# Summing the second layer's early partial attention groups with 32-column weights, under another table of planner thresholds

## The chip, the cores and the metric

The kernel runs on one core of one Trainium2 chip. The core has a matrix engine (TensorE, PE in the profile, its weight loads PEld), a vector engine (VectorE, DVE), an activation engine (ScalarE, ACT), a general engine (GpSimd, POOL) and a queue that issues transfers (SyncE, SP). The metric is device microseconds of one execution; the time of a kernel is the median of its runs.

## The reference

Four layers on 2048 tokens of width 512, all in bfloat16, each added to its input after a layer norm: A, B, A, B. Both kinds have 32 heads of width 16.

```
A: per segment of 512 tokens: p = softmax(causal(q k^T / 4)); a_dot = p v
   o = sigmoid(beta) * a_mem + (1 - sigmoid(beta)) * a_dot
   a_mem = (phi(q) M) / (phi(q) z); then M += phi(k)^T v, z += sum phi(k)
B: p = softmax(q k^T / 4) over all 2048 keys; o = p v
x = x + A(ln(x)); x = x + B(ln(x)); x = x + A(ln(x)); x = x + B(ln(x))
```

## The kernel before

The whole program is written by a planner (`Builder`) that runs before the launch. It keeps an estimated clock for each engine (`Sched.estimate`, line 95), decides from these clocks what to issue next, and so fixes the order of the instructions on every engine; on the chip each engine works through its list and waits on semaphores. Layers are numbered L = 0 to 3; 0 and 2 are of kind A, 1 and 3 of kind B.

**Groups and banks.** Attention is cut into groups (`Group`, made in `make_groups`, line 1363): one layer, one segment of 512 queries, one chunk of 8 heads, and every second head of it (`e` is 0 or 1), so 4 heads. Scores are made as blocks of 128 keys by 512 queries of one head, one PSUM bank each (the code calls the pair of key block and head a bank): 64 for a whole group of kind B. In layer 1 the groups of the first query segment (`qseg` 0) are cut into four waves, one for each key segment, of 16 banks each, since the keys of later segments come late out of layer 0. That makes 32 partial groups, which run in three stretches between the segments of layer 0. Layer 3 cuts its first query segment into two waves in the same way.

**A unit** (`unit`, line 1454) takes two or three banks. TensorE makes the scores with 32-row weights (four heads lie in four row strips: tiles `ps<-qm,KB`), ScalarE takes the exponential of two or three banks in one instruction into `pT` (line 1514), and two units later TensorE multiplies the exponentials with the values and sums over keys into one accumulator bank (`pv`, line 1556). The values have 16 columns and a column of ones, so the sum of the exponentials comes out as the 17th.

**The share of VectorE.** For some banks the exponential is approximated on VectorE instead: one eviction to 16-bit integers (`dx_first`, line 1121) and two or three shifts of these (`dx_shift`, line 1184), each of which gives one more term that `pv` must sum. Which banks go this way, when, and in what order is decided by thresholds of the planner (`dx_room`, `dx_find`, `dx_most`).

**Two forms of the sum.** In the narrow form the exponentials are the weights (128 by 128) and the values stream, so that a bank takes four matmuls of 50 or 52 columns, with the queries on the partitions; a finished group is divided by its sums, written to `ob` and brought to `oT` by a DMA transpose. In the wide form (`g.fm`) the values are the weights (17 columns, in a 32-column strip of the array that is picked by the head's place `r`), the exponentials stream, and a bank takes one matmul of 512 columns; queries lie on the free axis, and VectorE transposes the finished sums in blocks of 32 (`finish_fm`, line 1634) and transposes the output of two groups again into `oT` (line 1674). The form is picked by

```
self.fm = kind == "B" and Builder.FM >= (1 if L == 3 and first and last else
          2 if L == 3 else 3 if first and last else 4)                 # line 252
```

With `FM` = 3 all of layer 3 and the whole groups of layer 1 (query segments 1 to 3) are wide; the 32 partial groups of layer 1 are narrow.

**Partial sums** (`finish`, line 1592). At the end of each wave the accumulator is added by VectorE into an SBUF area (`accS`: tiles `KB` or `VB`): a copy at the first wave (line 1604), an addition after (line 1606), over 272 columns in the narrow form and 512 in the wide one. Until it has been read, the next group's sums cannot start in the accumulator.

**Background.** Layer norms, projections, output projections and the memory of kind A are tasks that the planner slips between units (`background`, line 1316) by credits and by how far each engine's clock is ahead. Projections go through one PSUM bank, which ScalarE or VectorE evicts (`evac`, line 475). Where TensorE has little to do, `keep_busy` (line 429) adds matmuls of zeros.

**The table.** `PIECES` (line 271) is a list of times on the planner's ScalarE clock, one each 40 us from 20 us on; when the clock passes a time, the thresholds named there are set (line 1810) and hold until they are set again. Among them are how many banks VectorE may take (`TAKEN`, `REST`, `NEAR_S`), how far clocks may drift (`MARGIN`, `SLACK`, `DVE_LATE`), the credits per unit (`CR_W`, `PE_B`) and the zeros (`FILL`, `FILLS`).

Of the kernel before, what the change touches and what calls it, by code (L numbers as in the profile page):

```python
# [257 lines left out]
class Builder:  # L258
    NPU, NDX, FIT, MARGIN, PART, FILL_DVE, EARLY, FILL = 4, 5, 2, 450, 1, 300, 700, 0.5
    FILLS, DVE_FIN, DX_FIN, EVAC_ACT, DX_BANK, DX_LATE, BG_BANK, DVE_LATE = 2, 600, 2000, 0, 500, 3000, 200, 1000  # L260
    DVE_LATE_LOW, CR_A, CR_B, CR_W, CR_LOW, CARRY, CARRY_W, REST = 9000000000.0, 1300, 1500, 1400, 1900, 0, 0, 11
    NEAR, SLACK, ALT3, ALT5, GAP, AHEAD, PE_B, PE_A = 10, 300, 2, 4, 2, 300, 4, 5
    PE_LOW, LOW, PAIRS, TAKEN, PAIRS2, NKS, DX_T, POOL_T = 6, 24, 40, 2.7, 1, 6, 430, 2900
    POOL_ON, DQN, TAKEN_N, REST_N, NEAR_N, NEAR_W, DQ, DXS = 0, 600, 3, 14, 130, 8, 2200, 1
    PVN, PVLATE, PVWAIT, PVHOLE, DMA_STEPS, DMA_LATE, DXA, DXA_REST = 4, 900, 0, 100, 2, 600, 0, 10
    DXA_N, DXA_W, APARTS, FILL_NEAR, FILL_FREE, HOR, PHI, QUAD = 13, ('k0', 'k13'), ('k2', 'k13', 'k0'), 0, 1, 400, 'kq', ('in', 1, 3)
    QREST, CLOSE, FM, NAREA, XDX, NEAR_S, NEAR_E, DX_WAIT = 24, ('proj', 2, 2), 3, 18, 99, 60, 60, 400
    DX_RES, CHAINS, ALT, ALTS, ALTA = 0, 4, 0, 3, (1, 1, 1, 1)
    ORDER = [[(-4.6, 7.7, 7.6, 0.9, -10), (3.8, -10.8, 0.4, 20, -10.8), (19, 59.6, 22, 59.8, 12), (31, 44.3, 46.9, 10.6, 0.2)],
             [(-1.5, -6.7, -5.8, 20.8, 1.2), (-5.2, -1.6, 28.5, 28, 7), (21, 35.0, 8.2, 30, 27.7), (21, 48.0, 37, 23.6, 12.2)]]  # L270
    PIECES = [(20.0, {'DXA_REST': 14, 'EVAC_ACT': -300, 'LOW': 32}),
              (60.0, {'AHEAD': 500, 'CR_W': 1900, 'DXA_REST': 10, 'EVAC_ACT': -300, 'LOW': 24, 'wide': True}),
              (100.0, {'AHEAD': 500, 'CR_W': 1900, 'DQ': 1900, 'EVAC_ACT': -300, 'wide': True}),
              (140.0, {'AHEAD': 300, 'CR_W': 1400, 'DQ': 2200, 'DX_T': 480, 'EVAC_ACT': 0}),
              (180.0, {'DMA_LATE': 300, 'DX_FIN': 2500, 'DX_T': 480, 'PE_B': 5, 'PE_LOW': 5}),
              (220.0, {'DMA_LATE': 600, 'DX_FIN': 2000, 'DX_T': 430, 'LOW': 16, 'PE_B': 4, 'PE_LOW': 6, 'PVN': 6}),
              (260.0, {'DX_RES': 2, 'HOR': 100, 'LOW': 24, 'NEAR_N': 200, 'PVN': 4}),
              (300.0, {'DX_RES': 2, 'HOR': 100, 'MARGIN': 700, 'NEAR_N': 200}),
              (340.0, {'DMA_LATE': 300, 'DQ': 1900, 'DX_RES': 2, 'FILLS': 1, 'HOR': 100, 'MARGIN': 700, 'NEAR_E': 80, 'NEAR_N': 200}),
              (380.0, {'DMA_LATE': 300, 'DMA_STEPS': 3, 'DQ': 2500, 'DX_RES': 2, 'DX_T': 330, 'FILLS': 1, 'HOR': 100, 'MARGIN': 700, 'NEAR_E': 0, 'NEAR_N': 200}),  # L280
              (420.0, {'DMA_LATE': 300, 'DMA_STEPS': 3, 'DQ': 2500, 'DX_RES': 2, 'DX_T': 330, 'FILLS': 1, 'HOR': 100, 'MARGIN': 700, 'NEAR': 6, 'NEAR_E': 0, 'NEAR_N': 200}),
              (460.0, {'ALTA': (1, 9, 9, 9), 'DMA_LATE': 300, 'DMA_STEPS': 3, 'DQ': 2500, 'DX_RES': 2, 'DX_T': 330, 'FILLS': 1, 'HOR': 100, 'MARGIN': 700, 'NEAR': 10, 'NEAR_E': 0, 'NEAR_N': 200, 'TAKEN': 1.5}),
              (500.0, {'ALTA': (1, 1, 9, 9), 'CR_W': 1250, 'DMA_LATE': 600, 'DMA_STEPS': 2, 'DQ': 2200, 'DQN': 300, 'DX_RES': 0, 'DX_T': 430, 'FILLS': 2, 'HOR': 400, 'MARGIN': 450, 'NEAR_E': 60, 'NEAR_N': 130, 'TAKEN': 2.7}),
              (540.0, {'ALTA': (1, 1, 1, 1), 'CR_W': 1400, 'DQ': 2500, 'DQN': 600, 'PE_A': 4}),
              (580.0, {'DQ': 2200, 'FILLS': 1, 'FILL_DVE': 450, 'PART': 3, 'PE_A': 5}),
              (620.0, {'FILLS': 1, 'FILL_DVE': 450, 'NEAR_S': 30, 'PART': 3, 'SLACK': 150}),
              (660.0, {'FILLS': 2, 'FILL_DVE': 300, 'NEAR_S': 60, 'PART': 1, 'SLACK': 0}),
              (700.0, {'MARGIN': 700, 'SLACK': 0, 'TAKEN': 2.4}),
              (740.0, {'DQ': 2500, 'DX_LATE': 1500, 'MARGIN': 700, 'SLACK': 0, 'TAKEN': 2.4}),
              (780.0, {'DQ': 2200, 'DX_LATE': 3000, 'MARGIN': 450, 'PVHOLE': 250, 'PVLATE': 600, 'SLACK': 300, 'TAKEN': 2.7}),  # L290
              (820.0, {'BG_BANK': 0, 'PVHOLE': 100, 'PVLATE': 900, 'TAKEN': 3}),
              (860.0, {'AHEAD': 200, 'BG_BANK': 200, 'TAKEN': 2.7}),
              (900.0, {'AHEAD': 200, 'DX_LATE': 1500, 'DX_RES': 1}),
              (940.0, {'AHEAD': 200, 'DX_LATE': 1500, 'DX_RES': 1, 'FILL_DVE': 150, 'MARGIN': 700}),
              (980.0, {'AHEAD': 200, 'DX_LATE': 1500, 'DX_RES': 1, 'FILL_DVE': 150, 'MARGIN': 700, 'REST': 14}),
              (1020.0, {'AHEAD': 200, 'DVE_FIN': 1000, 'DX_LATE': 1500, 'DX_RES': 1, 'FILL_DVE': 150, 'MARGIN': 700, 'PART': 3, 'REST': 14}),
              (1060.0, {'AHEAD': 300, 'CARRY_W': 300, 'DVE_FIN': 600, 'DX_LATE': 3000, 'DX_RES': 0, 'FILL': 0.35, 'FILL_DVE': 300, 'MARGIN': 450, 'PART': 1, 'REST': 11, 'REST_N': 20}),
              (1100.0, {'CARRY_W': 300, 'DMA_STEPS': 3, 'DXA_REST': 26, 'FILL': 0.35, 'LOW': 4, 'REST_N': 20}),
              (1140.0, {'CARRY_W': 0, 'DMA_STEPS': 2, 'DXA_REST': 10, 'FILL': 0.5, 'FILLS': 3, 'LOW': 4, 'PVN': 3, 'REST_N': 14}),
              (1180.0, {'FILLS': 3, 'LOW': 4, 'NEAR_S': 30, 'PVN': 2}),  # L300
              (1220.0, {'FILLS': 3, 'LOW': 4, 'MARGIN': 700, 'NEAR_S': 30, 'PVN': 2}),
              (1260.0, {'DVE_FIN': 1000, 'FILLS': 3, 'LOW': 4, 'MARGIN': 700, 'NEAR_S': 30, 'PVN': 2}),
              (1300.0, {'AHEAD': 200, 'BG_BANK': 400, 'DVE_FIN': 1000, 'DX_RES': 1, 'FILLS': 3, 'FILL_DVE': 150, 'LOW': 4, 'MARGIN': 700, 'NEAR_S': 30, 'PVN': 2}),
              (1340.0, {'AHEAD': 200, 'BG_BANK': 400, 'DVE_FIN': 1000, 'DX_RES': 1, 'FILL': 0.45, 'FILLS': 3, 'FILL_DVE': 150, 'LOW': 4, 'MARGIN': 700, 'NEAR_S': 30, 'PVN': 2}),
              (1380.0, {'AHEAD': 200, 'BG_BANK': 400, 'DVE_FIN': 1000, 'DX_RES': 1, 'FILL': 0.45, 'FILLS': 3, 'FILL_DVE': 150, 'LOW': 4, 'MARGIN': 700, 'NEAR_S': 30, 'PVN': 2}),
              (1420.0, {'AHEAD': 200, 'BG_BANK': 400, 'DVE_FIN': 1000, 'DX_RES': 1, 'FILL': 0.45, 'FILLS': 3, 'FILL_DVE': 150, 'LOW': 4, 'MARGIN': 700, 'NEAR_S': 30, 'PVN': 2}),
              (1460.0, {'AHEAD': 200, 'BG_BANK': 400, 'DVE_FIN': 1000, 'DX_RES': 1, 'EVAC_ACT': -300, 'FILL': 0.45, 'FILLS': 2, 'FILL_DVE': 150, 'LOW': 4, 'MARGIN': 700, 'NEAR_S': 30, 'PVN': 2, 'REST': 14, 'REST_N': 20}),
              (1500.0, {'AHEAD': 200, 'BG_BANK': 400, 'DVE_FIN': 1000, 'DX_RES': 1, 'EVAC_ACT': -300, 'FILL': 0.45, 'FILL_DVE': 150, 'LOW': 4, 'MARGIN': 700, 'NEAR_S': 30, 'PVN': 2, 'REST': 14, 'REST_N': 20}),
              (1540.0, {'AHEAD': 200, 'BG_BANK': 400, 'DVE_FIN': 1000, 'DX_RES': 1, 'EVAC_ACT': -300, 'FILL': 0.45, 'FILL_DVE': 150, 'LOW': 4, 'MARGIN': 700, 'NEAR_S': 30, 'PVN': 2, 'REST': 11, 'REST_N': 20}),
              (1580.0, {'AHEAD': 200, 'BG_BANK': 400, 'DVE_FIN': 1000, 'DX_RES': 0, 'EVAC_ACT': -300, 'FILL': 0.45, 'FILL_DVE': 150, 'LOW': 4, 'MARGIN': 700, 'NEAR_S': 30, 'PVN': 2, 'REST': 5, 'REST_N': 20, 'TAKEN': 3.5}),  # L310
              (1620.0, {'AHEAD': 200, 'BG_BANK': 400, 'DVE_FIN': 1000, 'EVAC_ACT': -300, 'FILL': 0.45, 'FILL_DVE': 150, 'LOW': 4, 'MARGIN': 700, 'NEAR_S': 30, 'PVN': 2, 'REST': 5, 'REST_N': 20, 'TAKEN': 3.5}),
              (1660.0, {'AHEAD': 300, 'BG_BANK': 200, 'DVE_FIN': 600, 'DX_T': 530, 'EVAC_ACT': 0, 'FILL': 0.5, 'FILL_DVE': 300, 'LOW': 24, 'MARGIN': 450, 'NEAR_N': 200, 'NEAR_S': 60, 'PVN': 4, 'REST': 11, 'REST_N': 14, 'TAKEN': 3, 'TAKEN_N': 4}),
              (1700.0, {'DVE_FIN': 1000, 'DX_T': 530, 'NEAR_N': 200, 'TAKEN': 3, 'TAKEN_N': 4}),
              (1740.0, {'DVE_FIN': 1000, 'DX_T': 530, 'NEAR_N': 200, 'REST': 8, 'TAKEN': 3, 'TAKEN_N': 4})]


    def __init__(self, nc, A_x, A_wq, A_wk, A_wv, A_wo, A_beta, B_x, B_wqkv, B_wo, out):
# [1568 lines left out]
```

## Time and profile before

| | |
|---|---|
| runs | 1776.07, 1779.52, 1780.4 us; median 1779.52 |
| profiled execution | 1777.42 us, of which 1775.7 us from the first to the last instruction |
| mean granted TensorE clock | 0.989 |
| busy | PE 1586.7 us, DVE 1520.6 us, ACT 1733.2 us, POOL 287.4 us |
| instructions of layer 1 with narrow weights `ps<-VB,pT` | 1788 matmuls |
| partial sums, lines 1604 and 1606 | 16 copies and 40 additions |

Rows of the profile read: line of the source, engine, operation, tile written<-tiles read, shape, count, then busy time and mean nanoseconds of one, then the idle time of the engine just before these instructions and what ended it.

### The profile page before, as it was taken

How to read it: one execution, taken by the hardware profiler on the slowest of the kernel's cores; microseconds unless marked ns; L12 is line 12 of the kernel's file. 1: busy time of each engine (PE TensorE's matmuls, PEld its weight loads, DVE VectorE, ACT ScalarE, POOL GpSimd, SP SyncE). 2: the span in 40 equal slices, each digit the busy share in tenths (PEclk: the TensorE clock that was granted, in tenths of full speed). 3: DMA queues.
4: the chain of work that ended last, by engine and by line, in shares of the span. 5: the costliest groups of instructions: out<-in, count | busy, mean ns of one | idle time of the engine just before them, and what ended most of it. 6: DMA issues, size and time to landing. Idle time of an engine off the chain costs nothing.

```text
span 1775.7 us, 42674 instructions
## 1 busy us (share of the span) xinstructions
PE 1586.7 (89%) x17429; PEld 564.7 (32%) x17429; DVE 1520.6 (86%) x3016; ACT 1733.2 (98%) x1680; POOL 287.4 (16%) x656
## 2 busy tenths in 40 slices
PE   8889899999998999999999989999888888888887
PEld 4445454452223222323222332332222222222222
DVE  6677867499985999798999789767999999999998
ACT  7999999999999999999999999999999999999998
POOL 4622415110005000203000330241100000000000
PEclk9999999999999999999999999999999999999999
DMA  6121111000101000000000010010000000000000
GB/s 173 22 47 32 29 17 26 14 12 4 16 7 16 1 13 13 8 13 19 1 13 13 16 23 13 16 22 13 2 13 1 1 1 13 1 1 7 7 1 13
DMA packets 86180, 30.01 MB, mean 17 GB/s; under 512 B 78816, under 2 KB 85472, under 8 KB 85984
## 3 DMA queue, kind: packets, MB, share of 16 engines
q1 hardware_dynamic: 85984, 27.29, 7.5%
q8 instruction: 136, 2.23, 0.5%
q14 instruction: 60, 0.49, 0.1%
HBM read 6.30 MB, written 2.10 MB: 5 GB/s over the span
## 4 chain that ended last, share of the span: by engine, by line
ACT 50%; PE 22%; issue 16%; DVE 9%; POOL 2%; DMA 1%; SPq 0%; ACTq 0%; DVEq 0%; POOLq 0%
ACT pT L1514 49%; PE ps L445 22%; POOL pT L1529 2%; DVE KB L1121 1%; DVE VB L1121 1%; DVE dxw L1184 1%; ACT amem L697 0%; DVE dxw L1121 0%; DVE QA L1121 0%; DMA xT<-xn 0%; DVE KA L1121 0%; DVE KA L1646 0%; DVE KB L1184 0%; DVE x L911 0%; DVE VB L1184 0%
## 5 line engine op out<-in xcount | busy, mean ns | idle before, releaser
L1514 ACT ACTIVATE pT<-ps 128x1024 bf16<-128x1024 f32 (+4 forms) x1627 | 1700.1, 1193 | 27.9 <-PE ps L445 19.8
L445 PE MATMUL ps<-qm,KB 32*128 32x512 bf16 x3584 | 524.0, 386 | 97.8 <-ACT pT L1514 87.0
L445 PE MATMUL ps<-pT,VB 128*17 128x512 bf16 x2217 | 378.9, 387 | 10.5 <-ACT pT L1514 6.0
L1529 POOL TENSOR_SCALAR_AFFINE_SELECT pT<-pT 128x256 bf16<-128x256 bf16 (+2 forms) x524 | 211.8, 416 | 545.0 <-ACT pT L1514 533.0
L445 PEld LDWEIGHTS ps<-qm,KB 32*128 32x128 bf16 x3584 | 132.3, 91 | 465.7 <-ACT pT L1514 360.5
L1424 POOL TENSOR_SCALAR qm<-QB,par 128x512 bf16<-128x512 bf16 x88 | 68.2, 777 | 856.4 <-PE ps L445 782.8
L445 PEld LDWEIGHTS ps<-pT,VB 128*17 128x17 bf16 x2217 | 87.6, 87 | 244.2 <-issue 198.9
L1121 DVE TENSOR_SCALAR dxw<-ps 128x512 uint16<-128x512 f32 (+1 forms) x209 | 143.6, 698 | 5.3 <-PE ps L445 4.4
L445 PE MATMUL ps<-qm,QA 32*128 32x512 bf16 x512 | 111.4, 391 | 25.4 <-ACT pT L1514 22.7
L1184 DVE TENSOR_SCALAR dxw<-dxw 128x1024 uint16<-128x1024 uint16 (+1 forms) x315 | 125.2, 409 | 3.0 <-PE ps L445 1.3
L1121 DVE TENSOR_SCALAR QA<-ps 128x512 uint16<-128x512 f32 (+1 forms) x174 | 122.2, 715 | 5.4 <-PE ps L445 4.8
L445 PE MATMUL ps<-qm,KA 32*128 32x384 bf16 (+3 forms) x1024 | 103.4, 307 | 24.2 <-ACT pT L1514 20.0
L445 PE MATMUL ps<-VA,pT 128*128 128x51 bf16 (+1 forms) x2560 | 109.0, 189 | 14.0 <-POOL pT L1529 6.4
L1121 DVE TENSOR_SCALAR VA<-ps 128x512 uint16<-128x512 f32 (+1 forms) x159 | 114.0, 730 | 6.3 <-PE ps L445 5.5
L445 PE MATMUL ps<-dxw,VW 128*17 128x512 bf16 x435 | 110.6, 383 | 0.2 <-DVE dxw L1184 0.2
L445 PEld LDWEIGHTS ps<-VA,pT 128*128 128x128 bf16 x2560 | 86.2, 97 | 63.2 <-POOL pT L1529 29.7
L1121 DVE TENSOR_SCALAR KB<-ps 128x512 uint16<-128x512 f32 (+1 forms) x128 | 96.2, 769 | 2.8 <-PE ps L445 1.9
L445 PE MATMUL ps<-xT,wA 128*128 128x512 bf16 (+1 forms) x281 | 78.3, 381 | 1.5 <-DVE xT L658 0.9
L445 PE MATMUL ps<-pT,VA 128*17 128x512 bf16 x393 | 78.6, 387 | 1.2 <-ACT pT L1514 0.9
L1121 DVE TENSOR_SCALAR VB<-ps 128x512 uint16<-128x512 f32 (+1 forms) x99 | 74.7, 769 | 3.2 <-PE ps L445 2.6
L445 PE MATMUL ps<-dxw,VB 128*17 128x512 bf16 x256 | 74.3, 381 | 0.0
L445 PE MATMUL ps<-VB,pT 128*128 128x34 bf16 (+1 forms) x1788 | 69.5, 186 | 1.4 <-ACT pT L1514 1.1
(289 smaller groups left out, 2436.1 us busy)
## 6 DMA issues: line engine op xcount, KB each, us to landing
out_dram<-x SPq DMA_DIRECT2D x8, 256.0 KB, 2.2
x<-in_A_x_dram SPq DMA_DIRECT2D x3, 512.0 KB, 5.1
wB<-in_B_wqkv_dram SPq DMA_DIRECT2D x1, 1536.0 KB, 11.7
xT<-xn SPq DMA_TRANSPOSE x60, 2.4
oT<-ob SPq DMA_TRANSPOSE x36, 2.4
x<-in_A_x_dram SPq DMA_DIRECT2D x4, 128.0 KB, 2.3
wA<-in_A_wq_dram SPq DMA_DIRECT2D x1, 512.0 KB, 4.5
wA<-in_A_wk_dram SPq DMA_DIRECT2D x1, 512.0 KB, 6.1
```

The lines of the kernel that those rows point to most:

```text
L445: self.sc.add("pe", lambda e: e.matmul(out, lhsT, rhs, start=start, stop=stop, skip_group_check=True), reads=reads, banks=[(bank, "w", all ...
L1121: self.sc.add("dve", lambda e: e.tensor_scalar(d, o, SCALE * LOG2E * 128, W_C if dxs[0][:3] in self.wt else EXP_C, op0=ALU.mult, op1=ALU.add),
L1184: self.op("dve", lambda e: e.tensor_scalar(o, w, d, None, op0=ALU.add), reads=self.b_dxw[b0][:len(ents)], writes=wr, ns=(295, 425, 560, 69 ...
L1424: self.op(eng, (lambda m, q, col: lambda e: e.tensor_scalar(m, q, col, 0.0, op0=ALU.mult, op1=ALU.add))(m, q, col), reads=[bq, self.b_par] ...
L1514: self.sc.add("act", (lambda dst, src: lambda e: e.activation(dst, src, ACT.Exp, scale=SCALE))(dst, src), writes=self.b_pT[slot * 3 + i:sl ...
L1529: self.op("pool", (lambda blk, pat: lambda e: e.affine_select(blk, blk, pattern=pat, compare_op=ALU.is_ge, fill=0.0, base=0, channel_multi ...
```

## The change

`FM` goes from 3 to 4, so that the 32 partial groups of layer 1 take the wide form as well: in `pv`, in the width of the partial sums, and in `finish_fm` for the eight groups of the last wave. No other code is changed. Every row of `PIECES` is another one; the times stay, and the thresholds and the keys that rows name differ from the first row on. The lines of the diff, with the first and last rows of the table:

```diff
-    QREST, CLOSE, FM, NAREA, XDX, NEAR_S, NEAR_E, DX_WAIT = 24, ('proj', 2, 2), 3, 18, 99, 60, 60, 400
+    QREST, CLOSE, FM, NAREA, XDX, NEAR_S, NEAR_E, DX_WAIT = 24, ('proj', 2, 2), 4, 18, 99, 60, 60, 400
-    PIECES = [(20.0, {'DXA_REST': 14, 'EVAC_ACT': -300, 'LOW': 32}),
-              (60.0, {'AHEAD': 500, 'CR_W': 1900, 'DXA_REST': 10, 'EVAC_ACT': -300, 'LOW': 24, 'wide': True}),
+    PIECES = [(20.0, {'DX_FIN': 2500, 'GAP': 3, 'LOW': 32, 'NEAR_W': 48}),
+              (60.0, {'DQN': 1000, 'DX_FIN': 2000, 'EVAC_ACT': -300, 'GAP': 2, 'LOW': 24, 'NEAR_W': 8}),
...
-              (1700.0, {'DVE_FIN': 1000, 'DX_T': 530, 'NEAR_N': 200, 'TAKEN': 3, 'TAKEN_N': 4}),
-              (1740.0, {'DVE_FIN': 1000, 'DX_T': 530, 'NEAR_N': 200, 'REST': 8, 'TAKEN': 3, 'TAKEN_N': 4})]
+              (1700.0, {'DXA_REST': 10, 'DX_T': 430, 'EVAC_ACT': 0, 'FILL': 0.55, 'FILLS': 2, 'FILL_DVE': 300, 'FILL_NEAR': 0, 'HOR': 400, 'MARGIN': 450, 'NEAR_E': 60, 'PVHOLE': 100, 'QREST': 24, 'REST': 11, 'REST_N': 14}),
+              (1740.0, {'FILL': 0.5, 'QREST': 16})]
```

What the planner writes can be counted in the built program. In layer 1's first query segment: 2508 narrow matmuls fewer, 622 wide ones more, 30 matmuls of zeros in place of 12. Over the whole program the banks of ScalarE go from 3697 blocks of 512 columns to 3696, in 6 instructions fewer; VectorE's banks go from 1039 to 1040.

More of the change, by code (lines that the diff above doesn't have):

```diff
@@ L270 @@
              [(-1.5, -6.7, -5.8, 20.8, 1.2), (-5.2, -1.6, 28.5, 28, 7), (21, 35.0, 8.2, 30, 27.7), (21, 48.0, 37, 23.6, 12.2)]]
-    PIECES = [(20.0, {'DXA_REST': 14, 'EVAC_ACT': -300, 'LOW': 32}),
-              (60.0, {'AHEAD': 500, 'CR_W': 1900, 'DXA_REST': 10, 'EVAC_ACT': -300, 'LOW': 24, 'wide': True}),
[L273 to L312, printed above, removed]
-              (1700.0, {'DVE_FIN': 1000, 'DX_T': 530, 'NEAR_N': 200, 'TAKEN': 3, 'TAKEN_N': 4}),
-              (1740.0, {'DVE_FIN': 1000, 'DX_T': 530, 'NEAR_N': 200, 'REST': 8, 'TAKEN': 3, 'TAKEN_N': 4})]
```

40 lines of the change are left out of this document (added).

## The prediction

> **What bounds the kernel.** I read the page's busy times first, then the windows of busy time over stretches of the run.
>
> ```profile
> span 1775.7 us, 42674 instructions
> PE 1586.7 (89%) x17429; PEld 564.7 (32%) x17429; DVE 1520.6 (86%) x3016; ACT 1733.2 (98%) x1680; POOL 287.4 (16%) x656
> core 0: us, PE busy (x) PEld busy (x) DVE busy (x) ACT busy (x) POOL busy (x), PEclk, DMA share, GB/s
> 0.00:102.00 102.00, 86.73 (x1107) 45.25 (x1107) 65.53 (x181) 87.95 (x103) 54.97 (x143) 0.97 0.36 95
> 102.00:160.00 58.00, 53.74 (x872) 31.61 (x872) 46.25 (x112) 56.64 (x48) 5.28 (x9) 1.00 0.15 24
> ...
> 202.00:254.00 52.00, 48.85 (x873) 29.83 (x869) 39.09 (x94) 50.91 (x43) 5.53 (x8) 1.00 0.10 20
> 254.00:298.00 44.00, 38.31 (x536) 19.20 (x533) 28.37 (x63) 40.18 (x51) 27.02 (x67) 0.96 0.22 29
> 298.00:399.00 101.00, 93.44 (x1686) 54.94 (x1685) 72.19 (x152) 99.46 (x83) 14.54 (x23) 1.00 0.07 13
> 399.00:1760.00 1361.00, 1218.24 (x11775) 362.89 (x11771) 1228.79 (x2322) 1346.93 (x1302) 152.90 (x339) 0.99 0.05 10
> ```
>
> ScalarE is busy 98% of the span, so the time is its work plus the little that it waits. Following the built order's exponentials (line 1514) along the trace, the three stretches of the partial groups are 102 to 160, 202 to 254 and 298 to 399 us. What to see in the rows: the ACT column beside the length of each stretch. There ScalarE stands idle 1.4 + 1.1 + 1.5 = 4.0 us of 211: no gain on TensorE in these groups can be worth more. The rest of its 42.5 idle us lies elsewhere: 14.1 in the first 102 us, 3.8 between 254 and 298, 14.1 in all of 399 to 1760, most of what remains at the very end.
>
> **ScalarE's work, part by part.** Consecutive exponentials overlap in the records, so I price them by pitch and not by their means.
>
> ```profile
> L1514 ACT ACTIVATE pT<-ps 128x1536 bf16<-128x1536 f32 x606 | 872.1, 1501 | 16.3 <-PE ps L445 11.4 <-POOL pT L1529 1.8 <-POOL VB L882 0.9
> L1514 ACT ACTIVATE pT<-ps 128x1024 bf16<-128x1024 f32 x862 | 847.6, 1079 | 8.8 <-PE ps L445 6.4 <-POOL pT L1529 1.0 <-ACT pT L1514 0.2
> 338.63 5.50 ACT L1514 ACTIVATE pT<-ps 128x1536 bf16<-128x1536 f32 x4
> 1059.35 5.63 ACT L1514 ACTIVATE pT<-ps 128x1024 bf16<-128x1024 f32 x6
> ```
>
> Four of three banks take 5.50 us: (5.50 - 1.50) / 3 = 1.33 us each; six of two banks (5.63 - 1.08) / 5 = 0.91. A bank is 0.42 us and an instruction 0.07 on top. The built program has one bank and six instructions less: 0.42 + 6 x 0.07 = 0.8 us off. By the means (1501 less 1079 a bank, 235 ns on top) it would be 1.8. I take 0.8. In layer 1's first segment VectorE takes 61 banks, before 65: the room on TensorE is not turned into fewer exponentials.
>
> **TensorE in the three stretches.** Timeline rows: start, length, engine, work.
>
> ```profile
> 340.16 0.39 PE L445 MATMUL ps<-qm,KB 32*128 32x512 bf16 x3 [0.59 <-ACT pT L1514]
> 340.48 0.68 PE L445 MATMUL ps<-VB,pT 128*128 128x34 bf16 x20
> 341.00 1.02 PE L445 MATMUL ps<-wB,xT 128*128 128x512 bf16 x4
> 346.07 0.69 PE L445 MATMUL ps<-VB,pT 128*128 128x51 bf16 x20
> 346.69 0.39 PE L445 MATMUL ps<-qm,KB 32*128 32x512 bf16 x3
> 1088.79 0.39 PE L445 MATMUL ps<-pT,VB 128*17 128x512 bf16 x3
> 1088.80 0.39 PE L445 MATMUL ps<-dxw,VB 128*17 128x512 bf16 x1
> 1089.01 0.38 PE L445 MATMUL ps<-KB,VB 128*17 128x512 bf16 x2
> 1090.67 0.39 PE L445 MATMUL ps<-pT,VB 128*17 128x512 bf16 x2
> 1090.99 0.39 PE L445 MATMUL ps<-qm,KB 32*128 32x512 bf16 x1
> ```
>
> Twenty narrow matmuls run from 340.48 to 341.00: 0.026 us each. Wide ones of different strips start together (four at 1088.79 to 1088.80); the next turn starts 0.21 later. From scores to sums it is 0.32 (340.16 to 340.48), and from wide sums to scores 0.32 (1090.67 to 1090.99): 0.21 for the stream and 0.10 for the change of weight shape. From narrow to a projection no such 0.10 is seen; from narrow to scores, 346.07 to 346.69 less 20 x 0.026, it is 0.10.
>
> So a three-bank unit without a projection goes from 12 x 0.026 + 0.10 = 0.41 to 0.32; with a projection behind it, from 0.31 to 0.32. In sum: 2508 x 0.026 = 65 us go; 622 wide ones come, three to a turn 622 / 3 x 0.21 = 44 us (four to a turn 33, each alone 131); changes of shape in these units go from 304 to 383, 79 x 0.10 = 8 us; 18 more zeros at about 0.21, 4 us. I take 44, nearest to units of three heads: 9 us of TensorE less in 211 (ends: 20 less, 78 more).
>
> [...]
>
> And where ScalarE does wait in these stretches, the sums are not the cause:
>
> ```profile
> 342.13 0.69 DVE L480 CAST VB<-ps 128x512 bf16<-128x512 f32 x1 [2.16 <-PE ps L445]
> 342.88 0.55 PEld L445 LDWEIGHTS ps<-wB,xT 128*128 128x128 bf16 x4 [0.23 <-DVE VB L480]
> 344.38 1.45 ACT L1514 ACTIVATE pT<-ps 128x1536 bf16<-128x1536 f32 x1 [0.25 <-PE ps L445]
> ```
>
> A projection waits for the eviction of the one bank that projections have, the scores queue behind it, and ScalarE runs dry. A sum of 0.32 in place of 0.31 leaves that as it is. I credit a third of the 4.0 us: 1.4 off (ends 0 and 4.0).
>
> **VectorE, POOL and SP.**
>
> ```profile
> L1606 DVE TENSOR_TENSOR KB<-KB,ps 128x512 f32<-128x512 f32 x8 | 5.5, 684 | 1.2 <-PE ps L445 1.1
> L1606 DVE TENSOR_TENSOR KB<-KB,ps 128x272 f32<-128x272 f32 x12 | 5.2, 430 | 0.6 <-PE ps L445 0.3
> L1646 DVE STREAM_TRANSPOSE KA<-KB 128x512 f32<-128x512 f32 x4 | 2.8, 711 | 0.1
> L1674 DVE STREAM_TRANSPOSE oT<-KA 128x512 bf16<-128x512 bf16 x27 | 19.0, 704 | 0.3
> L1121 DVE TENSOR_SCALAR KB<-ps 128x1024 uint16<-128x1024 f32 x21 | 25.5, 1215 | 0.2 <-PE ps L445 0.2
> L1121 DVE TENSOR_SCALAR dxw<-ps 128x512 uint16<-128x512 f32 x203 | 136.3, 682 | 4.5 <-PE ps L445 3.7
> L1184 DVE TENSOR_SCALAR dxw<-dxw 128x1024 uint16<-128x1024 uint16 x271 | 112.6, 425 | 2.4 <-PE ps L445 1.3
> L1184 DVE TENSOR_SCALAR QA<-QA 128x2048 uint16<-128x2048 uint16 x48 | 32.7, 682 | 0.2 <-PE ps L445 0.2
> ```
>
> Each of 32 partial sums grows by 684 - 430 ns: 8.1 us. Eight last groups get a transpose, 8 x 0.71, their reciprocals and products as before: 5.7. Four output transposes, 4 x 0.70 = 2.8, replace four DMAs, so SP's queue only gets shorter. Evictions: 15 double ones more and 29 single ones fewer, 18.2 - 19.8 = -1.6. Shifts: 46 of two banks fewer, 19 of four more, 19.6 off and 13.0 on; the few other sizes I leave out. Four query masks move over from POOL and are left out too. About 8 us in all, of which 16.6 fall in stretches where VectorE is free for 11.8 + 12.9 + 28.8 = 53 us. That cover hides them; without it their price would pass to the projections' evictions, at most 16.6.
>
> The accumulator is held 0.25 us longer at 32 places, and TensorE's next sums and the scores behind them queue for it:
>
> ```profile
> L1606 DVE TENSOR_TENSOR KB<-KB,ps x20: 419/439/689, 211.4 to 1255.8; 128x272 f32<-128x272 f32 x12, 128x512 f32<-128x512 f32 x8
>   PEld ps L445: 4.2, 11
> ```
>
> Line 1606 has 40 instructions, and TensorE's weight loads waited 11 times for them. At that rate 32 x 11 / 40 x 0.25 = 2.2 us of TensorE (ends 0 and 8.1), below the 9 freed: nothing for ScalarE.
>
> **Sum.** 1777.42 (the profiled execution, 1.7 over its span) - 0.8 - 1.4 = 1775.2. The other 38 us of idle time are the new table's doing; the rows tell no direction, so I add 0. The profiled execution lies 2.1 under the median of the runs, so on their scale this is 1777.3; I say 1777. It is within 0.3%, 5.3 us, about what a measurement of this kernel can tell from no change.
>
> **Rivals.**
>
> *Faster: the new table empties waits elsewhere.* For it: 17.9 us stand idle from 254 to 298 and 399 to 1760, and every threshold there is new. Against it: ScalarE is already busy 1346.93 of 1361 us, 99%, so half of what is left must go. With 7 to 9 us less, the time is 1768 to 1770.
>
> *Slower: the granted clock drops where TensorE empties.* For it:
>
> ```profile
> 1040.00:1080.00 40.00, 36.27 (x351) 11.97 (x350) 38.50 (x82) 39.47 (x37) 4.28 (x7) 1.00 0.09 18
> 1080.00:1120.00 40.00, 36.42 (x282) 9.47 (x281) 36.72 (x86) 38.67 (x38) 0.71 (x1) 0.91 0.10 21
> 1160.00:1200.00 40.00, 35.92 (x376) 14.43 (x374) 24.29 (x56) 37.55 (x35) 13.81 (x31) 0.91 0.11 23
> 1094.49 0.60 PE L445 MATMUL ps<-pT,VB 128*17 128x512 bf16 x3
> ```
>
> At 0.91 the wide matmul takes 0.60 us and ScalarE idles 1.3 and 2.5 us in 40; at 1.00 beside it, 0.5. The three stretches run at 1.00 with narrow sums. If wide ones let them fall to 0.91, five windows of 40 us cost 0.8 to 2.0 each, 4 to 10 us: 1781 to 1787. It decides from a mean of about 0.92 there. Against it: 30 matmuls of zeros instead of 12, and wide sums are at 0.99 after 399. [...]
>
> *Slower: the new table leaves more waits from 399 on.* The same 14.1 us grown by half is 7: 1784.
>
> *The change does not do what it says.* The built program rules it out: no narrow sum of layer 1 is left.
>
> **Chances.** Forecast, within 5.3 us: 0.50. Faster by the table: 0.28. Slower: 0.22, of which 0.12 by the clock and 0.10 by the table. The range reaches past both, 1767 to 1787; the forecast's own, from the ends of its terms (1.8 and 4.0 us off at one end, 0.8 and nothing at the other, with the 2 us by which the runs before differ), is 1774 to 1781.
>
> **What would show it.** Right: 0.8 us less ScalarE pitch, idle in the three stretches between 0 and 4 us with clock 1.00, VectorE 16 us busier there. Wrong: ScalarE's idle time after 399 away from 14 by more than 5; a clock under 0.95 in a stretch; TensorE's waits for line 1606 several times larger and ScalarE's waits behind them.

## The result and the profile after

The changed kernel takes 1784.36 us (median of 20 runs, 1776.95 to 1788.25); the kernel before, run beside it, 1778.01 us. The ratio is 1.0035, 95% interval 1.0026 to 1.0043: 6.3 us slower, where no measurable change was forecast. The time lies inside the wide range, 1767 to 1787, and outside the forecast's own, 1774 to 1781.

The page's head and its busy times, after:

```profile
span 1786.3 us, 38509 instructions
PE 1572.0 (88%) x15293; PEld 503.7 (28%) x15466; DVE 1533.3 (86%) x2986; ACT 1733.7 (97%) x1674; POOL 284.7 (16%) x658
```

ScalarE still sets the time, and its busy time is what it was (1733.2 before). The profiled execution took 1788.06 us, and its span is 10.6 us longer than the one before; so the profiled pair shows 4 us more of a loss than the medians do. The windows of the changed kernel, cut where its three stretches of partial groups begin and end (length, then busy time of PE, PEld, DVE, ACT and POOL, granted clock, DMA share):

```profile
0.00:104.00 104.00, 85.09 (x1091) 45.00 (x1107) 66.27 (x181) 88.07 (x104) 54.93 (x143) 0.95 0.39 93
104.00:160.00 56.00, 49.83 (x415) 16.73 (x420) 46.35 (x110) 55.23 (x48) 5.16 (x8) 1.00 0.11 18
...
205.00:257.00 52.00, 46.99 (x401) 15.50 (x405) 42.32 (x101) 51.49 (x44) 5.40 (x8) 1.00 0.09 19
...
299.00:403.00 104.00, 89.91 (x705) 25.80 (x712) 76.71 (x154) 102.57 (x86) 15.21 (x24) 1.00 0.05 8
403.00:1770.00 1367.00, 1216.97 (x11598) 361.39 (x11716) 1233.80 (x2289) 1343.96 (x1291) 149.79 (x338) 0.99 0.05 9
```

Take the ACT column from the length of each stretch: the rest is idle time. In the three stretches ScalarE idles 0.8 + 0.5 + 1.4 = 2.7 us, 1.3 less than before, at clock 1.00. From 403 on it idles 23.0 us, where it idled 14.1: 9 us more, in stages that the change of form doesn't touch. The first 104 us add 1.9, the rest 0.5. With the 1.3 off, that is 10.1 of the 10.6 us; ScalarE's busy time adds 0.5.

Most of the 9 lies between 760 and 1320 us, where the second layer ends, the third is worked and the fourth begins. ScalarE's two main groups there, before and then after (the last part is the idle time ahead of them and what ended it):

```profile
L1514 ACT ACTIVATE pT<-ps 128x1024 bf16<-128x1024 f32 x296 | 287.3, 1066 | 4.8 <-PE ps L445 3.6 <-POOL pT L1529 0.4 <-ACT pT L1514 0.2
L1514 ACT ACTIVATE pT<-ps 128x1536 bf16<-128x1536 f32 x182 | 258.3, 1491 | 3.1 <-PE ps L445 2.9
```
```profile
L1514 ACT ACTIVATE pT<-ps 128x1024 bf16<-128x1024 f32 x286 | 275.2, 1071 | 6.5 <-PE ps L445 6.0
L1514 ACT ACTIVATE pT<-ps 128x1536 bf16<-128x1536 f32 x180 | 254.5, 1482 | 8.8 <-PE ps L445 8.4
```

7.9 us have become 15.3, and nearly all of it waits for scores from TensorE. One such place in the timeline of after, TensorE's rows and then ScalarE's:

```profile
912.57 0.39 PE L445 MATMUL ps<-wB,zero 128*128 128x512 bf16 x1
913.27 0.61 PE L445 MATMUL ps<-qm,KB 32*128 32x512 bf16 x3 [0.31 <-ACT pT L1514]
...
915.15 1.89 PE L445 MATMUL ps<-xT,wA 128*128 128x512 bf16 x4
...
918.65 1.45 ACT L1514 ACTIVATE pT<-ps 128x1536 bf16<-128x1536 f32 x1 [1.40 <-PE ps L445]
```

A 512-column matmul goes from 0.39 to 0.61 us, the window 910 to 920 has a granted clock of 0.66 (6.7 us of it at half clock), a projection of four matmuls takes 1.89 us, and the scores behind it come 1.40 us late.

### The profile page after: what moved, and what is told of

It reads as the page before. It is cut to its first block, busy times and chain, and to the rows that moved or that the text cites. A ratio compares the mean times of both kernels' runs of the same rounds, so it can differ in the third digit from the quotient of the medians.

```text
span 1786.3 us, 38509 instructions
## 1 busy us (share of the span) xinstructions
PE 1572.0 (88%) x15293; PEld 503.7 (28%) x15466; DVE 1533.3 (86%) x2986; ACT 1733.7 (97%) x1674; POOL 284.7 (16%) x658
## 4 chain that ended last, share of the span: by engine, by line
ACT 49%; PE 20%; issue 17%; DVE 12%; POOL 1%; DMA 0%; ACTq 0%; SPq 0%; DVEq 0%; POOLq 0%
ACT pT L1514 48%; PE ps L445 20%; DVE dxw L1121 1%; POOL pT L1529 1%; DVE dxw L1184 1%; DVE VB L1121 1%; DVE VA L1121 1%; ACT amem L697 1%; DVE KA L1646 0%; DVE phk L1121 0%; DVE ob L1628 0%; DVE lnst L582 0%; DVE xT L1121 0%; DVE QA L1121 0%; DVE QA L1184 0%
## 5 line engine op out<-in xcount | busy, mean ns | idle before, releaser
L1514 ACT ACTIVATE pT<-ps 128x1024 bf16<-128x1024 f32 (+4 forms) x1621 | 1700.8, 1205 | 37.7 <-PE ps L445 33.0
L445 PE MATMUL ps<-pT,VB 128*17 128x512 bf16 x2669 | 440.4, 385 | 14.3 <-ACT pT L1514 8.8
L1529 POOL TENSOR_SCALAR_AFFINE_SELECT pT<-pT 128x384 bf16<-128x384 bf16 (+2 forms) x530 | 212.6, 412 | 642.3 <-ACT pT L1514 628.9
L445 PEld LDWEIGHTS ps<-pT,VB 128*17 128x17 bf16 x2669 | 102.8, 87 | 289.0 <-issue 231.7
L1121 DVE TENSOR_SCALAR dxw<-ps 128x512 uint16<-128x512 f32 x231 | 154.5, 685 | 3.7 <-PE ps L445 3.2
L445 PE MATMUL ps<-dxw,VW 128*17 128x512 bf16 x563 | 131.4, 385 | 0.3 <-DVE dxw L1184 0.3
L1121 DVE TENSOR_SCALAR QA<-ps 128x512 uint16<-128x512 f32 (+1 forms) x158 | 112.2, 725 | 6.3 <-PE ps L445 5.0
L1121 DVE TENSOR_SCALAR VB<-ps 128x512 uint16<-128x512 f32 (+1 forms) x123 | 93.5, 783 | 2.7 <-PE ps L445 2.0
L1121 DVE TENSOR_SCALAR KB<-ps 128x512 uint16<-128x512 f32 (+1 forms) x113 | 85.5, 770 | 2.2 <-PE ps L445 1.6
L445 PE MATMUL ps<-dxw,VB 128*17 128x512 bf16 x305 | 83.2, 381 | 0.0
L445 PE MATMUL ps<-xT,wB 128*128 128x512 bf16 x228 | 64.4, 391 | 4.5 <-DVE ob L1628 2.1
```

What stands on the lines that cost most here:

```text
L445: self.sc.add("pe", lambda e: e.matmul(out, lhsT, rhs, start=start, stop=stop, skip_group_check=True), reads=reads, banks=[(bank, "w", all ...
L1121: self.sc.add("dve", lambda e: e.tensor_scalar(d, o, SCALE * LOG2E * 128, W_C if dxs[0][:3] in self.wt else EXP_C, op0=ALU.mult, op1=ALU.add),
L1514: self.sc.add("act", (lambda dst, src: lambda e: e.activation(dst, src, ACT.Exp, scale=SCALE))(dst, src), writes=self.b_pT[slot * 3 + i:sl ...
L1529: self.op("pool", (lambda blk, pat: lambda e: e.affine_select(blk, blk, pattern=pat, compare_op=ALU.is_ge, fill=0.0, base=0, channel_multi ...
```

## The experiments

For most runs I also give ScalarE's waits by pitch: the time from the end of one of its instructions to the end of the next, less the median of that distance for the same shape (0.92 us for two banks, 1.34 for three), summed over the profiled execution. 120 to 440 us holds the later part of the partial groups and what follows them. A profile is of one execution: that of e10 took 1793.74 us and that of e9 1794.65, each the longest of its six, so their waits are likely larger than those of a median execution.

| kernel | median, us | ratio (interval) | waits 120 to 440 | waits 760 to 1320 | all waits |
|---|---|---|---|---|---|
| before | 1778.0 | 1 | 12.4 | 13.3 | 50.0 |
| after | 1784.4 | 1.0035 (1.0026 to 1.0043) | 11.9 | 24.3 | 61.9 |
| e5: after, 98 more zeros | 1787.6 | 1.0055 (1.0042 to 1.0067) | 13.1 | 24.5 | 61.1 |
| e8: before, partial sums over 512 columns | 1777.5 | 1.0000 (0.9991 to 1.0010) | 13.5 | 14.6 | 50.3 |
| e9: order of before, wide sums | 1791.8 | 1.0076 (1.0057 to 1.0095) | 27.9 | 15.4 | 67.1 |
| e10: order of after, narrow sums | 1787.2 | 1.0062 (1.0043 to 1.0081) | 17.2 | 25.6 | 67.1 |
| e13: e9 and 136 more zeros | 1801.3 | 1.0133 (1.0115 to 1.0152) | 36.6 | 13.2 | 73.0 |
| e16: e9 and 47 more zeros | 1790.0 | 1.0074 (1.0056 to 1.0091) | 26.9 | 13.6 | 61.5 |
| e17: before, VectorE's part of the wide form alone | 1786.4 | 1.0057 (1.0036 to 1.0079) | 21.6 | 15.2 | 57.8 |
| e18: order of before, TensorE's part alone | 1776.2 | 0.9993 (0.9982 to 1.0004) | 13.3 | 11.9 | 48.1 |

**Form and table apart.** The two edits of the change, each alone (`FM` and the table decide together what the planner writes):

```diff
e1: FM 4, table of before
e2: FM 3, table of after
```

> The wide form alone: FM = 4 with the table of before. Its built program has 1024 banks on VectorE (before 1039) and 6.3 us more ScalarE work by pitch. Theory A (the wide form is harmless to TensorE and ScalarE in the three stretches, and the loss of the change sits in the new table): about before + 6 us, 1784, all of it the 15 lost banks, with ScalarE's waiting time like before's 50 us. Theory B (the wide form itself makes ScalarE wait, through the longer partial sums or the shape changes): more waiting in the three stretches, 1788 or above.

> The new table alone: FM = 3 with the table of after. Built: 1010 banks on VectorE, 12.1 us more ScalarE work than before. Theory A (loss in the new table): before + 12 for the banks + 6 or more for waits = 1796 or above. Theory B (loss in the wide form): no added waits, so before + 12 = 1790. If a table only fits the program that it was searched for, waits could rise further still.

e1 takes 1845.4 us, ratio 1.039 (1.037 to 1.041); e2 1843.3, 1.0381 (1.0364 to 1.0399). Each half alone costs some ten times what both do together, and far more than I had looked for (some 1784 to 1796, though upwards open). Then both forms with the same tables: with none, with one row that sets `MARGIN`, with one row that sets `LOW`.

```diff
-    PIECES = [(20.0, {...
+    PIECES = []
```

> FM = 3 and an empty table (the default thresholds throughout). Built: 1010 banks on VectorE, 11.1 us more ScalarE work than before. Control for the search: if waits are like before's, 1789; if the search of the table also bought fewer waits, more: 1795 to 1805.

> FM = 4 and an empty table. Built: 996 banks on VectorE, 6.5 us more ScalarE work than with FM = 3 and an empty table. The form without any searched table: Theory A gives e3 + 6.5; Theory B (form makes waits) gives e3 + 10 or more; if the wide form frees TensorE where ScalarE waits, e3 + 4 or less.

> FM = 3 with a table of one row that was not searched (MARGIN 700 throughout). Built: 991 banks on VectorE. With the next run a second pair of equal, unsearched tables, beside e3 and e4, whose difference was 5 us. By its ScalarE work, 21 us over before's, and waits like e3's: 1835 to 1845.

> FM = 4 with the same one-row table. Built: 985 banks on VectorE, 1.6 us more ScalarE work than e11. If the form costs the planner what e4 less e3 showed, e11 + 2 to + 7. If that difference was only the scatter between plans, it may come out on either side of e11.

> Narrow form, a table of one row, LOW 4 from 20 us on; 997 banks on VectorE, so some 42 banks' worth of 0.42 us more on ScalarE than before, with its waits like those of the kernels without a table: 1825 to 1845, ratio 1.027 to 1.038. It is the partner of the next run.

> The same table of one row with the wide form; 986 banks on VectorE, 4.4 us of exponentials more than its partner by pitch. Theory 'at an equal table the wide form costs time' (it did by 4.9 us without a table and by 29 us with MARGIN 700): 3 to 25 us over its partner. Rival 'it is chance which of two unsearched plans is better': within 3 us of its partner, or under it.

| table | narrow, us | wide, us | wide less narrow |
|---|---|---|---|
| none (e3, e4) | 1830.4 | 1835.3 | 4.9 |
| `MARGIN` 700 (e11, e12) | 1835.5 | 1865.0 | 29.4 |
| `LOW` 4 (e14, e15) | 1864.3 | 1872.3 | 8.0 |

So a table made for the other form (e1, e2) is worse than none (e3, e4): it fits the one program that it was searched for. Its effect can't be added to that of the form, and "which half of the change was it" has no answer in these runs. The wide form was the slower one under each equal table, though the intervals of the first and the third pair overlap (1.0278 to 1.0326 and 1.0303 to 1.0342; 1.0468 to 1.0519 and 1.0501 to 1.0555); e14 came out 20 us above what I expected of it, and e12 22 us. In all eight VectorE takes fewer banks than before's 1039 (1024 in e1, 985 to 1010 in the others), so their times also hold more exponentials.

**The granted clock.** The waits near 913 us suggested that TensorE, less busy in the new order (495.8 us of 760 to 1320 for 516.8 before), falls to half clock and is late for it. (In the record of the granted clock of both traces, before and after, every entry is 1.0 or 0.5; a half-clock stretch is one at 0.5; "zeros" are the matmuls of zeros that keep TensorE busy.) More zeros, with the order of everything else kept:

```diff
+        while m < 2 and sc.streamed(max(sc.t["pe"], at), 3413) + 213 * len(self.more) / 3413 < 0.5:
...
+            self.mm(self.ps[:, bank.col0:bank.col0 + 512], self.zero[:, :], self.wB[:, 0, 0:512], ..., "fill")
...
+            sc.t["pe"], sc.tiles, sc.streams = held
```

> The changed kernel with 98 more zero matmuls on TensorE (280 in place of 182, wherever the planner's own account of TensorE's activity over 3.4 us is below 0.5); every other instruction and its order are those of the changed kernel. Theory C (the new table lets TensorE fall idle, FILL being 0.35 in its rows from 740 to 1060 us, the granted clock halves, and ScalarE waits behind it): 4 to 8 us less than the changed kernel, so 0.999 to 1.001 of before. Theory A (the loss is in the order of the work that the table makes): no change, 1.003 to 1.004 of before.

> The changed kernel with 397 more zeros (579 in all, up to an activity of 0.6), the order otherwise unchanged. Theory C: half-clock stretches nearly gone, 6 to 12 us less than the changed kernel, unless the zeros, 0.21 us each, now stand in front of scores. Theory A: no gain, and a loss of some us from TensorE time spent on zeros: 1.003 to 1.008 of before.

> The kernel before with 335 more zeros (510 in all, up to an activity of 0.6), the order otherwise unchanged. Its profile has 9 half-clock stretches with about 14 us of ScalarE waits in and near them, the changed kernel's 9 with about 20. Theory C: 4 to 8 us less than before (0.996 to 0.998). Theory A: no gain, 1.000 to 1.003.

e5 raises the mean clock from 0.989 to 0.997, and of the waits between 30 us and ten before the end, those within and just behind half-clock stretches go from 18.4 to 4.2 us. The others go from 37.7 to 51.2: the sum stays, and the time is 1787.6. ScalarE's two groups of e5 over 760 to 1320 us show it, and the window of that stretch:

```profile
L1525 ACT ACTIVATE pT<-ps 128x1024 bf16<-128x1024 f32 x286 | 274.7, 1061 | 7.2 <-PE ps L456 6.3
L1525 ACT ACTIVATE pT<-ps 128x1536 bf16<-128x1536 f32 x179 | 252.2, 1473 | 6.1 <-PE ps L456 5.2 <-ACT pT L1525 0.2
```
```profile
760.00:1320.00 560.00, 508.98 (x4867) 164.14 (x4870) 474.00 (x970) 543.30 (x530) 99.27 (x226) 1.00 0.08 13
```

At clock 1.00 ScalarE still waits 13.3 us in its two groups (15.3 without the zeros, 7.9 before), and TensorE is busy 509 us for 496 (58 matmuls of the changed kernel are missing from its records there, which is part of the difference). More zeros only cost, and more than either theory had: e6, 1807.7 (1.0168, 1.0154 to 1.0182); e7, on the kernel before, 1793.7 (1.0093, 1.0080 to 1.0106). The half clock is how some of the waits look; lifting it with zeros gives nothing back.

The executions of one kernel say something on the clock too, since each has its own mean. The longer ones have the lower clock: the 20 of the changed kernel go from 1776.95 us at 0.997 to 1788.25 at 0.987, those of the kernel before, over all sessions, from 1770.88 at 0.997 to 1782.79 at 0.985, in both some 1.1 us for 0.001. Which of the two leads isn't shown by that. But at an equal 0.990 the medians are 1784.8 us (8 executions) and 1778.0 (16), so the loss of the change is no loss of mean clock; and e5, whose five executions all have 0.997, takes 1786.83 to 1788.58 us where the changed kernel's one execution at 0.997 took 1776.95. By that one execution, the 98 zeros cost some 10 us.

**VectorE's wider partial sums.** The kernel before, with the 32 additions and copies over 512 columns (nobody reads the 240 more):

```diff
-            a = a[:, 0:w]
+            acc, a = self.ps[:, bank.col0:bank.col0 + 512], a[:, 0:512]
```

> The kernel before, order unchanged, but the 32 partial sums of layer 1 copy or add 512 columns instead of 272 (the columns past 272 hold nothing that is used). This is 0.25 us more VectorE time at 32 places, with the accumulator held as much longer: the prediction's term of 8.1 us by itself. If free VectorE time hides it, as predicted: 0.999 to 1.001. If it holds up TensorE and the scores behind it: up to 1.0045.

1777.5 us, ratio 1.000: the 8.1 us on VectorE and the longer hold of the accumulator are hidden, as the prediction had it.

**Form and order exchanged.** Here the planner writes the one kernel's list, and the other's form is put in the place of each step: the order and zeros of before with wide sums (e9), the order and zeros of after with narrow sums (e10). The core of e9; e10 is its mirror image:

```diff
+        if g.swap:
+            self.instead(self.sc.ops["pe"][-4:], [lambda e: e.matmul(o, w, pT[:, 0:512], start=first, stop=last, skip_group_check=True)],
+                         [bp, parts[0][3]], bank)
...
-        w = 512 if g.fm else 16 * 17
+        w = 512 if g.fm or g.swap else 16 * 17
...
+            self.held("dve", a2.end, lambda: self.finish_fm(g, src, bsrc, bk, al))
```

> The planner runs exactly as in the kernel before (FM = 3, its table), so every unit, task and zero keeps its place; only what is emitted for layer 1's 32 partial groups is the wide form: one wide matmul where four narrow ones stood, partial sums over 512 columns, the last wave's transposes on VectorE in place of DMAs. This is the form's cost on the chip with nothing replanned. Theory A (the loss is in the new plan; the form itself is harmless or a small gain): 0.997 to 1.000 of before. Theory B (the form itself costs, by shape changes, strips that collide or partial sums): 1.002 to 1.006.

> The reverse: the planner runs exactly as in the changed kernel (FM = 4, the new table), and the 32 partial groups are emitted in the narrow form at the same places. Theory A: as slow as the changed kernel or some us slower, 1.0035 to 1.007 of before. Theory B: the loss goes, 0.999 to 1.002.

Both are slower than before, and the places differ. ScalarE's two groups over 760 to 1320 us, e9 and then e10:

```profile
L1516 ACT ACTIVATE pT<-ps 128x1024 bf16<-128x1024 f32 x286 | 277.3, 1063 | 5.1 <-PE ps L447 4.0 <-POOL pT L1531 0.4 <-ACT pT L1516 0.2
L1516 ACT ACTIVATE pT<-ps 128x1536 bf16<-128x1536 f32 x183 | 259.5, 1491 | 4.1 <-PE ps L447 3.7 <-issue 0.2
```
```profile
L1516 ACT ACTIVATE pT<-ps 128x1024 bf16<-128x1024 f32 x283 | 271.8, 1071 | 7.6 <-PE ps L447 6.5 <-POOL pT L1531 0.7
L1516 ACT ACTIVATE pT<-ps 128x1536 bf16<-128x1536 f32 x180 | 254.8, 1484 | 8.2 <-PE ps L447 7.8
```

Idle there: before 7.9, wide sums in before's order 9.2, after 15.3, narrow sums in after's order 15.8. The late waits go with the order, whichever form the early groups have: in the table above, three traces of the new order have 24.3 to 25.6 us of them, seven of the order of before 11.9 to 15.4. (Of the kernels in the order of before, only e7, with 335 more zeros, comes near: its two groups idle 14.8 us there.) The new order is what the planner writes with `FM` = 4 and the new table together; e1 and e2 show that it can't be put down to one of them. Early it is the other way round: waits of 120 to 440 us grow where form and order don't belong together (12.4 to 27.9 in before's order, 11.9 to 17.2 in after's, the latter in a long execution of e10).

**Is the wide form's price in before's order the clock?** In e9 the window of 360 to 420 us has a clock of 0.86, and the planner had put 12 zeros into the partial groups, for the narrow sums. Zeros were added at the units of the partial groups alone:

```diff
+        if g is not None and g.swap:
+            self.more_zeros(bank, al, own, n, at)
```

> The order of the kernel before, with the 32 partial groups of layer 1 summed in the wide form, and 136 more matmuls of zeros in the units of these groups (311 in place of 175); nothing else moves. The same without the zeros was 1791.8 us, ratio 1.008, with half-clock episodes at 276, 379, 389 and 410 us. Theory 'the form costs only through the clock': with TensorE kept active the episodes in the third stretch go, and the time comes back to 1776 to 1782, ratio 0.999 to 1.002; then the loss of the changed kernel is all in the order that its table gives. Rival 'the form costs by itself' (the change of weight shape, the longer hold of the accumulator): the episodes go and the ratio stays at 1.005 or more. Rival 'zeros cost what the clock gives': the waits only move, as in the run with 98 zeros, ratio 1.006 to 1.010.

> As the run with 136 zeros (order of the kernel before, wide sums for the 32 partial groups), with 47 more zeros in place of 136, at most one in 3.4 us. Without zeros it was 1791.8 us with 27.9 us of ScalarE's waits between 120 and 440 us, and with 136 zeros 1801 with 36.6; the kernel before has 12.4 there. Theory 'between the two lies a number that keeps the clock and costs little' (as the changed kernel with 30 zeros in its own order, 11.9): waits of 12 to 20 there, 1778 to 1786. Rival 'in this order the wide sums cost time with and without zeros': 25 us or more there, 1789 to 1800. Both expect the waits after 760 us as before, about 13 to 16 us up to 1320 and not the 24 of the changed kernel, since the order there is that of before.

With 136 zeros the granted clock of 360 to 440 us is 1.00, and the time is 1801.3, waits 36.6: the theory of the clock fell, and so did the range of the one that zeros cost what the clock gives; only "the form costs by itself" takes it in. With 47 it is 1790.0, 26.9. From 360 to 440 us ScalarE waits some 13 us in e13, whose clock is 1.00 there, some 12 in e16 and 1 in before. So the waits stand without a half clock too; how much of them the zeros make, these two runs don't tell, and the next two settle it.

**VectorE's and TensorE's part, each alone, in before's order.** e17 is e8 and 12 transposes of 0.71 us more in the eight last groups, with narrow sums. e18 is e9 with the wide matmuls alone, VectorE's steps and the DMA transposes as in the narrow form; it leaves out what would make an attention output of the wide sums.

```diff
e17:
+        if early:
+            self.more_tr(a, ba)
...
+        if early and g.e == 1:
+            self.more_tr(a, ba)
```
```diff
e18, against e9:
-        w = 512 if g.fm or g.swap else 16 * 17
+        w = 512 if g.fm else 16 * 17
...
-            self.held("dve", a2.end, lambda: self.finish_fm(g, src, bsrc, bk, al))
```

> The kernel before with narrow sums and all of VectorE's extra work of the wide form: the 32 partial sums over 512 columns (alone this was 1777.5 us, ratio 1.000) and 12 transposes of 0.71 us more in the eight last partial groups; TensorE and the order are as before. The 240 output columns that they add are read by nobody. Theory 'VectorE has the room', as the prediction had it: ratio 0.999 to 1.002. Rival 'the room of the third stretch lies where it isn't needed' (VectorE is busy 27.4 and 28.4 of 30 us in 360 to 420): the transposes, 8.5 us, come through in part, 3 to 8 us, 1781 to 1786.

> The order of the kernel before with the wide matmuls of the 32 partial groups on TensorE alone: VectorE adds 272 columns, divides, and the DMA transposes as in the narrow form, so that what it makes of the second layer's first segment is no attention output. Theory 'TensorE's part costs nothing but the clock': waits of ScalarE in 120 to 440 us of 15 to 20 us for 12.4 before, 1781 to 1786. Rival 'all of the cost is TensorE's' (the clock and the later start of the scores behind wide sums): 25 us or more there, 1789 to 1794, as with VectorE's part. If this is near 1778, all of the cost is VectorE's.

TensorE's part costs nothing: 1776.2 us, 0.9993 (0.9982 to 1.0004). VectorE's part costs 9.4 us, more than the 3 to 8 that I gave it: 1786.4, 1.0057 (1.0036 to 1.0079). Where, the windows of 360 to 420 us show, in the order before, e9, e17, e18, after:

```profile
360.00:420.00 60.00, 55.82 (x1007) 29.58 (x1006) 55.82 (x106) 59.49 (x54) 6.20 (x8) 1.00 0.07 11
```
```profile
360.00:420.00 60.00, 49.91 (x361) 11.80 (x358) 52.71 (x92) 49.16 (x42) 6.11 (x8) 0.86 0.00 1
```
```profile
360.00:420.00 60.00, 48.95 (x929) 29.30 (x934) 55.45 (x100) 51.89 (x45) 5.57 (x7) 0.94 0.06 11
```
```profile
360.00:420.00 60.00, 52.74 (x464) 14.21 (x466) 55.89 (x106) 59.34 (x54) 5.36 (x8) 1.00 0.06 10
```
```profile
360.00:420.00 60.00, 50.75 (x433) 13.83 (x437) 55.96 (x105) 59.24 (x52) 5.82 (x8) 1.00 0.01 1
```

ACT idles 0.5 us in before, 10.8 in e9, 8.1 in e17, 0.7 in e18 and 0.8 in after. e18 has the wide matmuls and before's zeros, and its clock is 1.00; e17 has the narrow ones and falls to 0.94. So it isn't the wide sums that bring the clock down in e9: the drop comes with VectorE's part. The chain, from 360 to 420 us: the transposes added in e17, then what TensorE's scores waited for, in before and in e17, then ScalarE's exponentials of three banks, in before and in e17 (these over 298 to 420):

```profile
L1567 DVE STREAM_TRANSPOSE KA<-VB 128x512 f32<-128x512 f32 x6 | 4.3, 709 | 0.1
L1567 DVE STREAM_TRANSPOSE KA<-KB 128x512 f32<-128x512 f32 x6 | 4.3, 709 | 0.1
```
```profile
L445 PE MATMUL ps<-qm,KB 32*128 32x512 bf16 x179 | 24.0, 384 | 3.9 <-ACT pT L1514 3.6
```
```profile
L445 PE MATMUL ps<-qm,KB 32*128 32x512 bf16 x152 | 21.9, 403 | 8.9 <-DVE VA L1121 3.4 <-ACT pT L1514 2.1 <-DVE dxw L1121 1.3
```
```profile
L1514 ACT ACTIVATE pT<-ps 128x1536 bf16<-128x1536 f32 x60 | 83.8, 1478 | 1.7 <-PE ps L445 1.1 <-POOL qm L1424 0.3
```
```profile
L1514 ACT ACTIVATE pT<-ps 128x1536 bf16<-128x1536 f32 x60 | 84.0, 1472 | 9.0 <-PE ps L445 8.6 <-POOL qm L1424 0.3
```

All 12 transposes, 8.6 us, fall into these 60 us, where VectorE of the kernel before was free for 60 - 55.82 = 4.2. Its evictions of score banks (line 1121) come late, TensorE's next scores need those banks, and ScalarE needs the scores. e9 lies 14.8 us over the runs of before beside it, the two parts alone 9.4 and -0.8 over theirs. The rest of some 6 goes along with the clock of e9's executions: four of its six have 0.983 to 0.985 and take 1791.8 to 1794.7 us, but the one at 0.990 takes 1785.35, as e17's at 0.990 does (1785.49).

## Why the prediction was wrong

**The step that failed** is "The other 38 us of idle time are the new table's doing; the rows tell no direction, so I add 0." That term measured +9.0 us from 403 us on and +2.4 before it, outside the three stretches, in the profiled execution, which shows 4 us more than the medians. e9 and e10 show that the later part belongs to the order that the planner writes with the new table, and not to the wide sums. What in that order makes TensorE's scores late stays open: e5 shows only that it isn't the half clock. The prediction's rival "the new table leaves more waits from 399 on" named this place, with a chance of 0.10, and put it at 1784; 1784.4 came. The place was right and had too little weight. That the number was met is luck: "grown by half" came from no row.

**A second step was wrong, in the order of before:** "That cover hides them", of VectorE's 16.6 us in 53 us of free time. For the 8.1 us of sums it held (e8). For the 8.5 us of transposes it doesn't hold in before's order (e17). I had taken the 28.8 free us of the third stretch as one; the finer windows of the kernel before show where they lie:

```profile
298.00:330.00 32.00, 30.24 (x531) 17.66 (x530) 23.40 (x60) 31.64 (x27) 6.27 (x12) 1.00 0.09 19
330.00:360.00 30.00, 27.41 (x381) 14.28 (x380) 13.25 (x25) 29.13 (x24) 2.91 (x4) 1.00 0.03 6
360.00:390.00 30.00, 27.85 (x601) 17.77 (x601) 27.44 (x50) 29.73 (x26) 3.98 (x5) 1.00 0.09 12
390.00:420.00 30.00, 27.97 (x413) 11.81 (x409) 28.39 (x57) 29.76 (x29) 2.22 (x3) 1.00 0.05 11
```

In 330 to 360 VectorE is free for 16.8 of 30 us, in 360 to 420 for 4.2 of 60, and the last wave ends behind 360. A share of busy time over 101 us said nothing of that; the profile of before could have told it. In before's order VectorE's part costs some 9 us, 7.6 of it in 360 to 420. The changed kernel doesn't pay this: in 360 to 420 its VectorE is busy 55.96 us, no more than before, with all 12 transposes in it, since the new order puts fewer evictions of score banks there: line 1121 evicts 36 banks (8 times two and 20 times one), before 48 (14 and 20). The first segment as a whole gives up four banks only, so most of this is when they are taken. So the second step has no share in the 6.3 us that is shown. That the waits from 403 us on are the price of the room is my reading and not shown; shown is that they are the order's. Whether some other table has neither was not tried on the chip.

**What was right.** The three stretches: idle 2.7 us for a forecast of 4.0 - 1.4 = 2.6, clock 1.00. That it is a third of the 4.0 was a guess that came out, and that the sums brought it is not shown: e18, with wide sums in before's order, idles 3.4 us from 102 to 160, 202 to 254 and 298 to 360, where before idles 3.7. TensorE there: 196.0 us in 211 before (53.74 + 48.85 + 93.44), 186.7 in 212 after, 9.3 less for a forecast of 9; some 16 of its 1537 matmuls there are missing from the records, worth 2 us, which leaves 7. ScalarE's own work: by pitch all its instructions come to about 1 us less, forecast 0.8. The accumulator's hold, in the rows of line 1606 before and after:

```profile
who waited for it (us, times):
  PEld ps L445: 4.2, 11
  PE ps L445: 0.4, 2
```
```profile
who waited for it (us, times):
  PEld ps L445: 5.6, 14
  PE ps L445: 1.7, 6
```

The weight loads' waits grow from 4.2 to 5.6 us and the matmuls' from 0.4 to 1.7, 2.7 together for a forecast of 2.2, and e8, with the longer hold alone, shows that nothing of it reaches ScalarE.

**What was off without moving the time.** The sum took 2.1 us from the median of three runs, 1779.52; over 20 runs the median of before is 1778.01, and on that scale the sum gives 1775.8 and not 1777.3. VectorE is busy 12.7 us more (1533.3 less 1520.6), forecast about 8. In the three stretches it is 165.4 us for 157.5, 7.9 more where I expected 16: that line counted what the new form adds and left out the banks that VectorE gives up there.

**The other rivals.** "The granted clock drops where TensorE empties" is decided by e18, wide sums with the 12 zeros of before: clock 1.00 from 360 to 420 us and no time lost. In the changed kernel itself the three stretches have 1.00, and the loss stands at equal mean clock. For a while e9's clock spoke for it, but e13 and e17 turned that round. "The new table empties waits elsewhere" had the right place and the wrong sign. That half of the forecast's cases lay within 0.3% rested on the 0 above; the measured 6.3 us lie just outside.

**No better version** came out. e18 says why, for the order of before: with VectorE's part left out altogether, the wide sums come to a ratio of 0.9993 (0.9982 to 1.0004). TensorE's 9 us are not on the path there, so there is nothing to win by paying VectorE for them.

## What to carry to other kernels

When a change gives one idle engine's time to another, look at the receiving engine in windows as short as the work that it gets, at the place where it gets it: in the order of before, 53 us free in three stretches hid 8 us of sums and not 8.5 us of transposes that fell into 60 us with 4.2 free. A table searched for one program is worth some 3% of the time to that program (1778.0 us with it and 1830.4 without, 1784.4 and 1835.3) and less than nothing to a near relative (e1, e2), so form and table are judged together, or by exchanging form and order with the other held fixed. And when two searched plans are compared, put the plan's own spread into the forecast: it was the largest term here and I had set it to 0.

## What the runs showed of the hardware

Half-clock stretches: the trace of before has seven of 3.41 us and two of 6.83, that of after six and three, and the end of each trace cuts off one more (at 1.1 and 1.3 us). Within each trace they begin whole multiples of 3.41 us apart; in after those at 769.91, 913.27 and 974.71 us lie 143.36 and 61.44 us apart, 42 and 18 times 3.413. TensorE needn't stand idle for such a stretch: behind the first 100 us of these two traces, and but for the one at the end, it is busy 53 to 79% of the 3.41 us ahead of each by its records, and its longest pause there is 0.78 us. A stretch can also come with a wait that it didn't begin: 12 VectorE transposes, with the wider partial sums that cost nothing alone (e8, ratio 1.000), took the clock from 1.00 to 0.94 in 60 us of e17 with TensorE's program unchanged. Zeros that raise the clock are not free: with 98 of them in e5 its mean went from 0.989 to 0.997, and the time from 1784.4 to 1787.6 us.
